# Attention plus soft mixture of experts on one core: the product p v in one PSUM area, the left-over keys in four 64x64 tiles, the keys' factor moved into the maximum's pass, and a plan with every engine strictly in order

## The chip, the core and the metric

One core of one Trainium2 chip runs the whole program. TensorE (PE) multiplies matrices, VectorE (DVE) and ScalarE (ACT) work on tiles, GpSimd (POOL) takes small helpers, and SyncE (SP) issues the DMAs. Results of TensorE land in PSUM, everything else lies in SBUF. The metric is the device time of one execution in microseconds; the median of three runs counts.

## The reference

The inputs are q, k and v of shape (8, 8, 576, 64): 8 batches of 8 heads. Attention keeps only the scores near each row's maximum, and its output, laid out as 4608 rows of 512, goes through a soft mixture of 8 experts with 4 slots each.

```python
scores = scale * q @ k.T                       # scale = 1/8
thresh = max(scores) - tau
scores = where(scores >= thresh, scores, -1e9)
attn = exp(scores - max(scores)); attn /= sum(attn) + 1e-9
x = attn @ v                                   # (4608, 512)
logits = x @ phi                               # 32 slots
d = softmax of logits over the rows;  slot_input = d.T @ x
slot_out[e] = relu(slot_input[e] @ w1[e]) @ w2[e]
out = (softmax of logits over the slots) @ slot_out
```

## The kernel before

**Pairs.** Two heads make a pair: 32 pairs, four to a batch. The head dimension is 64, so the two contraction halves of TensorE's array hold 64 rows each. A pair has nine score blocks (i = 0 to 8): eight of 128 queries of one head against its 576 keys, and a ninth with the last 64 queries of both heads. Line 552 issues a score block as two matmuls side by side, keys 0 to 287 in the upper and 288 to 575 in the lower half of the array (plan mode HALVES); line 557 issues the ninth as four matmuls of 64x64 tiles (mode QUADS).

**A block's way.** The keys have been multiplied by 1/8 (and by 0, if tau is negative) in SBUF by POOL (line 532; for the first pair by DVE in two halves). DVE's pass over the scores in PSUM (line 564) writes the negated scores to SBUF (ss) and accumulates the row's minimum of them (nmx, minus the maximum). ACT takes the exponential (574), POOL the threshold (577), and DVE's second pass (580) zeroes what lies under the threshold, and sums the row. TensorE transposes the result p in 64-row pieces (478, from the helper `ptr`), and ACT copies the transposed pieces to SBUF (483, from `act_copy`): pTa for queries 0 to 255, pTb for 256 to 575, pTl for the 64 left-over keys (512 to 575) of both heads.

**The product p v.** Line 670 makes it in two visits, one for pTa (256 columns) and one for pTb (320 columns). A visit has five steps for each head, the two heads side by side in column halves of the array (mode COLS): four of 128 keys, and a fifth, from pTl, in which 64 rows of vv are zeros, since pTl holds both heads' left-over keys in its 128 partitions. Each visit writes a PSUM area of its own; ACT copies it to xT, TensorE transposes that to x (`ptr`), POOL divides by the row sums (689), and TensorE transposes it back (694). After four pairs `dispatch` makes logits (752) and slot inputs (800, 805) for the batch.

**Areas.** PSUM is cut into four areas ps0 to ps3 of two banks; a score block, a block of transposes and a visit of p v take one each. pTa, pTb, pTl and pL exist once, k, q and vv twice, p2 (two score blocks' p) and ss four times.

**Order.** `Order.add` records every operation with a nominal time (a pair's start plus an entry of OFF or of TABLE), and `plan` turns them into one order per engine by simulating the engines with fixed costs. Before the change, an engine that can't start its first operation by nominal time takes the next one that it can. For TensorE a change of mode costs SWITCH.

**Weights.** 64 units of 512 KB feed the experts. NPRE of them are loaded during the pairs into areas of their own, 20 ("host") into SBUF that the pairs give back at their end, and the rest into areas that the first expert stage has read. SP issues all of them in order.

Of the kernel before, what the change touches and what calls it, by code (L numbers as in the profile page):

```python
# [1174 lines left out]
```

## Time and profile before

| | us |
|---|---|
| median of 3 runs | 548.01 |
| lowest, highest run | 547.24, 548.21 |
| span of the profiled execution, first to last instruction | 546.2 |
| TensorE busy in the span | 527.5 |
| VectorE busy in the span | 471.0 |
| ScalarE busy in the span | 457.4 |
| GpSimd busy in the span | 242.1 |

The profile gives the span of the execution that it took, and no other time of it; the median lies 1.8 us above that span, for what stands before the first and after the last instruction. The granted clock is 1.00 in every stretch until 530 us. From about 20 to 470 us the pairs run, and one batch of four pairs repeats itself every 57.6 us. From 464 to 513 us the weights stream in. A float32 matmul shows as two records, one for each of its two passes, so "x16" in a TensorE row is eight matmuls, that is four of each head.

### The profile page before, as it was taken

What the parts mean: (1) busy time and instruction counts of PE and PEld (TensorE: products, weight loads), DVE (VectorE), ACT (ScalarE), POOL (GpSimd) and SP (SyncE); (2) the same over time, 40 slices, a digit from 0 to 9 for tenths busy, and PEclk for the clock granted to TensorE, in tenths of its full rate; (3) what the DMA queues carried; (4) which work ended last, traced back from release to release, by engine and by line L of the source; (5) the groups of instructions that cost most, each with busy time, mean ns of one, the idle gap of its engine ahead of it and who ended that gap; (6) DMA issues with size and microseconds to landing.
All of it is one profiled execution on the core that took longest, in us unless ns stands there. A gap on an engine that the chain in (4) does not pass through costs nothing.

```text
span 546.2 us, 18324 instructions
## 1 busy us (share of the span) xinstructions
PE 527.5 (97%) x7029; PEld 337.0 (62%) x7029; DVE 471.0 (86%) x1332; ACT 457.4 (84%) x790; POOL 242.1 (44%) x475
## 2 busy tenths in 40 slices
PE   8999999999999999999999999999999999999990
PEld 6666666666666666666666666666666656644470
DVE  5999998999999999999899989999999999523192
ACT  3899998999899989999999989999999888621181
POOL 2554555554545464545355545545454524121030
PEclk9999999999999999999999999999999999999997
DMA  6355555565535543333333333333333322999498
GB/s 176 74 158 178 168 167 169 138 190 161 166 90 167 172 153 122 92 94 86 78 91 92 91 91 92 91 91 91 91 90 91 91 76 69 336 410 408 197 375 316
DMA packets 31990, 83.03 MB, mean 152 GB/s; under 512 B 4640, under 2 KB 12832, under 8 KB 31904
## 3 DMA queue, kind: packets, MB, share of 16 engines
q1 hardware_dynamic: 31904, 81.87, 48.8%
q8 instruction: 55, 0.90, 0.7%
q14 instruction: 31, 0.25, 0.2%
HBM read 72.42 MB, written 9.44 MB: 150 GB/s over the span
## 4 chain that ended last, share of the span: by engine, by line
PE 82%; DVE 5%; DMA 5%; ACT 4%; issue 2%; DVEq 0%; POOL 0%; SPq 0%; POOLq 0%; ACTq 0%
PE ps L670 29%; PE ps L552 24%; PE ps L478 17%; DMA w<-in_w 5%; PE ps L557 3%; PE ps L694 2%; PE ps L752 2%; PE ps L800 1%; DVE p L580 1%; PE up L418 1%; DVE cT L989 1%; DVE host L1086 1%; ACT pTa L483 1%; DVE ss L564 1%; PE ps L470 1%
## 5 line engine op out<-in xcount | busy, mean ns | idle before, releaser
L564 DVE TENSOR_SCALAR_CACHE_REDUCE ss<-ps 128x576 f32<-128x576 f32 x288 | 209.1, 752 | 15.5 <-ACT pTl L483 4.8
L577 POOL TENSOR_SCALAR thr<-nmx,pabs 128x1 f32<-128x1 f32 x288 | 132.2, 461 | 187.0 <-DVE ss L564 167.7
L580 DVE SCALAR_TENSOR_TENSOR p<-ss,thr,p 128x576 f32<-128x576 f32 x256 | 201.8, 823 | 3.4 <-ACT p L574 3.1
L574 ACT ACTIVATE p<-ss,nmx 128x576 f32<-128x576 f32 x256 | 188.2, 781 | 18.3 <-DVE ss L564 18.2
L552 PE MATMUL ps<-k,q 64*128 64x288 f32 x1024 | 167.2, 427 | 1.0 <-ACT pTb L483 0.4
L478 PE MATMUL ps<-ident,p 64*128 64x64 f32 x2304 | 98.2, 223 | 0.9 <-ACT pTa L483 0.3
L478 PEld LDWEIGHTS ps<-ident,p 64*128 64x128 f32 x2304 | 87.8, 138 | 17.8 <-issue 3.3
L552 PEld LDWEIGHTS ps<-k,q 64*128 64x128 f32 x1024 | 83.3, 188 | 21.9 <-ACT pTl L652 5.8
L483 ACT COPY pTb<-ps 128x1024 f32<-128x1024 f32 (+1 forms) x96 | 84.0, 876 | 5.7 <-PE ps L478 3.5
L670 PE MATMUL ps<-pTb,vv 128*64 128x320 f32 x512 | 76.0, 439 | 0.4 <-DVE pTl L652 0.4
L483 ACT COPY pTa<-ps 128x1024 f32<-128x1024 f32 x64 | 64.9, 1018 | 0.4 <-PE ps L478 0.4
L670 PE MATMUL ps<-pTa,vv 128*64 128x256 f32 x512 | 62.3, 385 | 0.0
L670 PEld LDWEIGHTS ps<-pTb,vv 128*64 128x64 f32 x512 | 34.1, 136 | 36.4 <-issue 9.0
L670 PEld LDWEIGHTS ps<-pTa,vv 128*64 128x64 f32 x512 | 33.9, 136 | 26.2 <-DVE ss L564 8.5
L670 PE MATMUL ps<-pTl,vv 128*64 128x256 f32 (+1 forms) x256 | 41.9, 406 | 0.0
L689 POOL TENSOR_TENSOR x<-x,ri 128x512 f32<-128x512 f32 x31 | 32.3, 1043 | 4.8 <-ACT x L483 4.8
L483 ACT COPY xT<-ps 128x256 f32<-128x256 f32 (+1 forms) x62 | 24.6, 398 | 6.2 <-PE ps L670 5.2
L670 PEld LDWEIGHTS ps<-pTl,vv 128*64 128x64 f32 x256 | 18.5, 137 | 12.6
L580 DVE SCALAR_TENSOR_TENSOR pL<-ss,thr,pL 128x576 f32<-128x576 f32 x32 | 26.0, 812 | 0.0
L574 ACT ACTIVATE pL<-ss,nmx 128x576 f32<-128x576 f32 x32 | 24.8, 776 | 0.4 <-DVE ss L564 0.4
L954 POOL TENSOR_TENSOR c<-lall,crow 128x512 f32<-128x512 f32 x9 | 9.3, 1046 | 35.7 <-PE ct L470 21.4
L483 ACT COPY pTl<-ps 128x256 f32<-128x256 f32 x64 | 24.2, 378 | 0.4 <-PE ps L478 0.4
(165 smaller groups left out, 550.3 us busy)
## 6 DMA issues: line engine op xcount, KB each, us to landing
w<-in_w SPq DMA_DIRECT2D x44, 512.0 KB, 7.3
q<-in_qT SPq DMA_DIRECT2D x62, 288.0 KB, 4.5
vv<-in_vt SPq DMA_DIRECT2D x32, 320.0 KB, 4.6
host<-in_w SPq DMA_DIRECT2D x20, 512.0 KB, 7.8
k<-in_kT SPq DMA_DIRECT2D x62, 144.0 KB, 3.0
out<-w SPq DMA_DIRECT2D x8, 512.0 KB, 3.4
out<-host SPq DMA_DIRECT2D x8, 512.0 KB, 5.0
out<-host SPq DMA_DIRECT2D x4, 256.0 KB, 4.6
```

The lines of the kernel that those rows point to most:

```text
L478: nc.tensor.transpose(out=s[:, g, c:c + 64], in_=ins[g], identity=ident[rows[g], rows[g]], tile_position=(64 * g, 0))
L483: G.add("ACT", 51 + 0.833 * n, nom, lambda: nc.scalar.copy(*io()), r, w)
L552: nc.tensor.matmul(s.t[:, g, 0:HS], qt.t[rows[g], h, c * 128:(c + 1) * 128], kt.t[rows[g], h * HS:(h + 1) * HS], start=True, stop=True, ti ...
L557: nc.tensor.matmul(s.t[rows[a], g, 0:HS], qt.t[rows[g], a, SM:S], kt.t[rows[g], a * HS:(a + 1) * HS], start=True, stop=True, tile_position ...
L564: dve(674, t + OFF['mx'], [s], [ss, nmx], lambda s=s, ss=ss, nmx=nmx: nc.vector.tensor_scalar(out=ss.t.rearrange("p (a k) -> p a k", a=2), ...
L574: G.add("ACT", 668, t + OFF['ex'], lambda sv=sv, nmx=nmx, view=view: nc.scalar.activation(view().rearrange("p (a k) -> p a k", a=2), sv(), ...
L577: pool(250, t + OFF['th'], lambda nmx=nmx, thr=thr: nc.gpsimd.tensor_scalar(out=thr.t, in0=nmx.t, scalar1=1.0, scalar2=pabs, op0=ALU.mult, ...
L580: fn=lambda sv=sv, thr=thr, view=view, i=i: nc.vector.scalar_tensor_tensor(out=view().rearrange("p (a k) -> p a k", a=2), in0=sv(), scalar ...
L670: nc.tensor.matmul(lone(w)[h * 64:(h + 1) * 64, 0:n], vv.t[:, v0:v0 + 64], p0, start=(kb == 0), stop=(kb == 4), tile_position=(0, h * 64), ...
L689: G.add("POOL", 1040, u + 6.8, own=f"new{j}", r=[ri[0]], w=[x[j]], fn=lambda: nc.gpsimd.tensor_tensor(out=wide(), in0=wide(), in1=ri.t[:, ...
L694: nc.tensor.transpose(out=w.t[:, g, c * 64:c * 64 + 64], in_=xj()[rows[g], c], identity=ident[rows[g], rows[g]], tile_position=(64 * g, 0))
L752: nc.tensor.matmul(lone(wl)[c * 32:(c + 1) * 32, o], phi_sb[:, k, :], xT[k].t[:, q(c)], start=(k == 0 and not o.start), stop=(k == HP - 1) ...
```

## The change

- **Left-over keys.** The fifth step of p v goes. Instead four matmuls of 64x64 tiles follow the second visit (line 695 of the changed kernel), one for each head and each of two query ranges (256 and 320 columns), in mode QUADS. For that the order of the two heads' left-over keys is swapped for queries from 256 on, keys and p are laid out anew (`kt` is 128 x 2 x 352 now, `at` places a block in p2), and vv's left-over rows are loaded into both halves of the partitions.
- **One area.** Both visits write one PSUM area `o`, one bank each, and it is held from the first visit to the two copies to xT behind the QUADS. pTa and pTb become five slots of pT, one per 128 queries (four used by a pair), and pTL for the last 64 queries: the visits' matmuls have 128 and 64 columns in place of 256 and 320.
- **The factor.** POOL's pass over the keys goes (and DVE's two for the first pair). The maximum's pass multiplies by `nflag8`, a value per partition read from SBUF (minus 1/8, or 0), where it multiplied by the constant -1.0.
- **The plan.** Every engine but SP takes its operations strictly by nominal time. A change of mode costs 92 + 54, and a score behind anything that isn't a score 54 more. The ninth block moves ahead of the last two of the others. All table entries are new.
- **Loads.** A pair's keys come by three DMAs in place of two, its values by three in place of one. NPRE is 25 in place of 26.

```diff
-NPRE = 26
+NPRE = 25
...
-        -279.31, -244.60, -253.66, -174.00, -228.72, -214.94, -219.66, -331.57, -213.22, -305.02, -252.11, -385.08, 317.82, -201.86,
+        -28.68, -46.27, -46.24, -48.35, None, -11.70, -20.09, -3.47, None, 8.91, 2.93, -1.85, 1.91, -4.79, 4.95, 4.82, 4.73,
...
-    k=2, q=2, vv=2, r=3, ri=3, nmx=4, thr=4, p2=4, pL=1, pTa=1, pTb=1, pTl=1, l4=1,
+    k=2, q=2, vv=2, r=3, ri=3, nmx=4, thr=4, p2=4, pL=1, pT=5, pTL=1, pTl=1, l4=1,
...
+                if head[eng] < len(line[eng]):
+                    i = line[eng][head[eng]]
+                    if i in arrived and fits(i, eng):
+                        got = i
+                        head[eng] += 1
...
-                    end += SWITCH * (o[5] != mode) + 50 * (engfree[eng] < t)
+                    end += SWITCH * (o[5] != mode) + LEAD * (o[5] != mode or o[8] and not score) + 50 * (engfree[eng] < t)
...
-            sc = lambda e, kc=kc: lambda: e.tensor_scalar(out=kt.t[:, kc], in0=kt.t[:, kc], scalar1=flag8, **one)
-            if p == 0:
-                G.add("DVE", 370, t0 - 9 + hs[0], sc(nc.vector), [], [kt[h] for h in hs])
-            else:
-                pool(730, t0 - 9, sc(nc.gpsimd), [], [kt[h] for h in hs])
...
             dve(674, t + OFF['mx'], [s], [ss, nmx], lambda s=s, ss=ss, nmx=nmx: nc.vector.tensor_scalar(
-                out=ss.t.rearrange("p (a k) -> p a k", a=2), in0=s.t[:, :, 0:HS], scalar1=-1.0, scalar2=3.4028234663852886e38,
+                out=ss.t.rearrange("p (a k) -> p a k", a=2), in0=s.t[:, :, 0:HS], scalar1=nflag8, scalar2=3.4028234663852886e38,
                 op0=ALU.mult, op1=ALU.min, accum_out=nmx.t))
...
-                for kb in range(5):
-                    for h in range(2):
-                        v0, p0 = ((h * 4 + kb) * 64, pT.t[:, h, kb, :]) if kb < 4 else (SM + h * 64, pTl.t[:, q])
-                        nc.tensor.matmul(
-                            lone(w)[h * 64:(h + 1) * 64, 0:n], vv.t[:, v0:v0 + 64], p0,
-                            start=(kb == 0), stop=(kb == 4), tile_position=(0, h * 64), skip_group_check=True)
+        o = Buf("s")
+        for cs in ((0, 1), (2, 3, 4)):
+            part = [(pT[c], c, 128, c % 2 * 128) if c < 4 else (pTL, c, SL, 256) for c in cs]
+
+            def mm(part=part, k=cs[0] // 2):
+                for z, c, n, m in part:
+                    for kb in range(4):
+                        for h in range(2):
+                            nc.tensor.matmul(
+                                o.t[rows[h], k, m:m + n], vv.t[:, (h * 4 + kb) * 64:][:, 0:64], z.t[:, h, kb, :],
+                                start=(kb == 0 and not m), stop=False, tile_position=(0, h * 64), skip_group_check=True)
...
+        def mm():
+            for k in range(2):
+                for h in range(2):
+                    q = slice(0, QA) if k == 0 else slice(QA, S)
+                    g = h ^ k
+                    nc.tensor.matmul(
+                        o.t[rows[h], k, 0:q.stop - q.start], vv.t[rows[g], SM + h * 64:][:, 0:64], pTl.t[rows[g], q],
+                        start=False, stop=True, tile_position=(64 * g, 64 * h), skip_group_check=True)
```

TensorE's order at the second visit of p v in a pair in the middle of the run, from the first visit on, before. L670 is p v, L552 a score block, L478 transposes, L694 the transposes of x back, and ps0 to ps3 are the PSUM areas:

```order
L670 MATMUL ps2_337<-pTa0_244,vv1_200 64x256 x8
L670 MATMUL ps2_337<-pTl0_208,vv1_200 64x256 x2
L552 MATMUL ps0_335<-k0_312,q0_316 128x288 x2
L478 MATMUL ps1_336<-ident_61,xT0_180 128x64 x8
L552 MATMUL ps2_337<-k0_312,q0_316 128x288 x2
L552 MATMUL ps3_338<-k0_312,q0_316 128x288 x2
L478 MATMUL ps1_336<-ident_61,p22_284 128x64 x16
L552 MATMUL ps0_335<-k0_312,q0_316 128x288 x2
L670 MATMUL ps2_337<-pTb0_204,vv1_200 64x320 x8
L670 MATMUL ps2_337<-pTl0_208,vv1_200 64x320 x2
L694 MATMUL ps0_335<-ident_61,x0_152 128x64 x8
L478 MATMUL ps1_336<-ident_61,p22_284 128x64 x2
```

The same place now, from the second half of the first visit to the transposes of xT. L684 is p v, L695 the four left-over matmuls, L569 a score block, L481 transposes:

```order
L684 MATMUL ps2_352<-pT1_295,vv1_199 64x128 x8
L569 MATMUL ps0_350<-k0_331,q0_335 128x288 x2
L569 MATMUL ps1_351<-k0_331,q0_335 128x288 x2
L481 MATMUL ps3_353<-ident_61,p22_255 128x64 x16
L684 MATMUL ps2_352<-pT0_207,vv1_199 64x128 x8
L684 MATMUL ps2_352<-pT4_223,vv1_199 64x128 x8
L684 MATMUL ps2_352<-pTL0_215,vv1_199 64x64 x8
L695 MATMUL ps2_352<-pTl0_203,vv1_199 64x256 x2
L695 MATMUL ps2_352<-pTl0_203,vv1_199 64x320 x2
L481 MATMUL ps0_350<-ident_61,p21_231 128x64 x16
L569 MATMUL ps1_351<-k1_311,q1_315 128x288 x2
L481 MATMUL ps2_352<-ident_61,xT1_183 128x64 x8
```

The area ps2 now holds the product through both visits and is taken again by the transposes of xT a block of transposes and a score block later; before, it was free between the visits and took a score block there.

VectorE's order where a pair begins, before. L564 is the maximum's pass, L580 the second pass, L618 the reciprocals of the row sums:

```order
L564 TENSOR_SCALAR ss3_196,nmx2_264<-ps2_337 128x576
L618 RECIPROCAL ri2_304<-ri2_304 128x8
L564 TENSOR_SCALAR ss0_216,nmx0_268<-ps1_336 128x576
L564 TENSOR_SCALAR ss2_252,nmx3_300<-ps3_338 128x576
L564 TENSOR_SCALAR ss1_240,nmx1_256<-ps2_337 128x576
L580 SCALAR_TENSOR_TENSOR p22_284,r0_308<-ss3_196,thr2_248,p22_284 128x576
```

And now (L581 is the maximum's pass, L597 the second pass):

```order
L581 TENSOR_SCALAR ss1_275,nmx3_287<-ps2_352,nflag8_78 128x576
L581 TENSOR_SCALAR ss2_243,nmx0_307<-ps0_350,nflag8_78 128x576
L581 TENSOR_SCALAR ss0_267,nmx2_303<-ps2_352,nflag8_78 128x576
L597 SCALAR_TENSOR_TENSOR p22_255,r0_319<-ss1_275,thr3_291,p22_255 128x576
L581 TENSOR_SCALAR ss3_195,nmx1_299<-ps0_350,nflag8_78 128x576
L581 TENSOR_SCALAR ss1_275,nmx3_287<-ps2_352,nflag8_78 128x576
```

The maximum's pass has a second input, nflag8, and a pair's first scores take turns on two areas, ps2 and ps0, where they took three.

## Rows read from the trace of the kernel before

**Rows 1.** The page's span and busy times: time, share of the span, instructions.
```profile
span 546.2 us, 18324 instructions
PE 527.5 (97%) x7029; PEld 337.0 (62%) x7029; DVE 471.0 (86%) x1332; ACT 457.4 (84%) x790; POOL 242.1 (44%) x475
```

**Rows 2.** Busy time by stretch, one batch of pairs and two stretches of the end: stretch, its length, busy time (instructions) of TensorE, its weight loads, VectorE, ScalarE and GpSimd, then granted clock, DMA share and GB/s.
```profile
297.20:354.80 57.60, 57.57 (x820) 37.45 (x818) 54.91 (x158) 54.57 (x95) 28.95 (x56) 1.00 0.34 86
470.00:490.00 20.00, 19.23 (x265) 10.82 (x263) 6.33 (x26) 5.75 (x15) 3.63 (x19) 1.00 1.02 404
490.00:510.00 20.00, 20.00 (x208) 7.83 (x204) 4.29 (x12) 3.37 (x8) 2.05 (x2) 1.00 1.03 410
```

**Rows 3.** The page's chain of work that ended last, as shares of the span: by engine, then by engine, tile and line.
```profile
PE 82%; DVE 5%; DMA 5%; ACT 4%; issue 2%; DVEq 0%; POOL 0%; SPq 0%; POOLq 0%; ACTq 0%
PE ps L670 29%; PE ps L552 24%; PE ps L478 17%; DMA w<-in_w 5%; PE ps L557 3%; PE ps L694 2%; PE ps L752 2%; PE ps L800 1%; DVE p L580 1%; PE up L418 1%; DVE cT L989 1%; DVE host L1086 1%; ACT pTa L483 1%; DVE ss L564 1%; PE ps L470 1%
```

**Rows 4.** TensorE in order of time, a pair and a half in the middle of the run, then two later rows of the same kind: start, duration, line, operation, tiles, array tile and shape, records. A group's own length is best read as the step from its start to the next group's start, since the duration includes the way of the last columns through the array.
```profile
242.84 2.37 PE L670 MATMUL ps<-pTb,vv 128*64 128x320 f32 x16
245.04 0.71 PE L670 MATMUL ps<-pTl,vv 128*64 128x320 f32 x4
245.68 0.46 PE L694 MATMUL ps<-ident,x 64*128 64x64 f32 x8
...
246.60 0.70 PE L552 MATMUL ps<-k,q 64*128 64x288 f32 x4
247.14 0.65 PE L478 MATMUL ps<-ident,p 64*128 64x64 f32 x16
247.63 1.68 PE L552 MATMUL ps<-k,q 64*128 64x288 f32 x12
249.14 0.47 PE L478 MATMUL ps<-ident,pL 64*128 64x64 f32 x10
...
249.58 0.70 PE L552 MATMUL ps<-k,q 64*128 64x288 f32 x4
250.21 1.95 PE L670 MATMUL ps<-pTa,vv 128*64 128x256 f32 x16
251.99 0.60 PE L670 MATMUL ps<-pTl,vv 128*64 128x256 f32 x4
252.52 0.71 PE L478 MATMUL ps<-ident,p 64*128 64x64 f32 x16
...
253.95 0.72 PE L557 MATMUL ps<-k,q 64*64 64x288 f32 x8
254.60 1.24 PE L552 MATMUL ps<-k,q 64*128 64x288 f32 x8
...
289.11 0.71 PE L670 MATMUL ps<-pTl,vv 128*64 128x320 f32 x4
...
302.66 0.71 PE L670 MATMUL ps<-pTl,vv 128*64 128x320 f32 x4
```

**Rows 5.** VectorE in order of time where it doesn't wait: the maximum's pass and the second pass, start and duration.
```profile
279.40 0.75 DVE L564 TENSOR_SCALAR_CACHE_REDUCE ss<-ps 128x576 f32<-128x576 f32 x1
...
280.08 0.75 DVE L564 TENSOR_SCALAR_CACHE_REDUCE ss<-ps 128x576 f32<-128x576 f32 x1
...
280.76 0.81 DVE L580 SCALAR_TENSOR_TENSOR p<-ss,thr,p 128x576 f32<-128x576 f32 x1
...
281.50 0.81 DVE L580 SCALAR_TENSOR_TENSOR p<-ss,thr,p 128x576 f32<-128x576 f32 x1
```

**Rows 6.** Three VectorE instructions of one element per partition at the program's start, each by its line: duration in ns (smallest, median, largest). Lines 392 and 409 have constants alone; line 407 (`scalar2=tau_sb`) reads a value per partition.
```profile
L392 DVE TENSOR_SCALAR flag<-tau_sb x1: 153/153/153, 3.3 to 3.3; 128x1 f32<-128x1 f32 x1
L407 DVE TENSOR_SCALAR nabs<-tau_sb x1: 203/203/203, 3.4 to 3.4; 128x1 f32<-128x1 f32 x1
L409 DVE TENSOR_SCALAR pabs<-nabs x1: 153/153/153, 3.6 to 3.6; 128x1 f32<-128x1 f32 x1
```

**Rows 7.** Groups of instructions by line and shape: out and in (partitions x elements), count, then busy us, mean ns of one, and the engine's idle time before them. Lines 1058 and 1063 both take two tensors of 256 columns; 1063 (`scalar=neg`) also reads a value per partition.
```profile
L564 DVE TENSOR_SCALAR_CACHE_REDUCE ss<-ps 128x576 f32<-128x576 f32 x288 | 209.1, 752 | 15.5 <-ACT pTl L483 4.8 <-PE ps L552 4.2 <-ACT pTa L483 1.9
...
L532 POOL TENSOR_SCALAR k<-k,flag 128x576 f32<-128x576 f32 x31 | 24.2, 780 | 0.7 <-DMA k<-in_kT 0.3
...
L1063 DVE SCALAR_TENSOR_TENSOR sh<-sh,neg,sr 128x256 fp32r<-128x256 f32 x2 | 1.0, 481 | 0.7 <-ACT sh L1062 0.6
...
L532 DVE TENSOR_SCALAR k<-k,flag 128x288 f32<-128x288 f32 x2 | 0.7, 370 | 2.7 <-DMA k<-in_kT 2.7
...
L1058 DVE TENSOR_TENSOR so_sb<-h00e,so_sb 128x256 f32<-128x256 f32 x1 | 0.4, 425 | 9.4 <-issue 9.4
```

**Rows 8.** SP's issues of weight loads at the end of the run: start, time from first to last of the group, line, number.
```profile
453.82 18.90 SPq L460 DMA_DIRECT2D host<-in_w  x12
475.39 5.39 SPq L458 DMA_DIRECT2D host<-in_w  x6
485.40 18.39 SPq L460 DMA_DIRECT2D w<-in_w  x18
```

**Rows 9.** Four pieces of the chain that ended last, in order of time: start, length, what.
```profile
39.28 0.74 DVE p L580 x2
...
439.49 0.82 DVE p L580 x3
...
503.45 10.09 DMA w<-in_w
...
513.58 0.83 PE h00e L1032 x9
```

More of the change, by code (lines that the diff above doesn't have):

```diff
@@ L28 @@
 HALVES, COLS, COLS4, QUADS, WHOLE = range(5)
-SWITCH = 145
+SWITCH = 92
+LEAD = 54
 REGIONS = 4
-NPRE = 26
+NPRE = 25
 UP = 22
@@ L166, in skip, with add @@
         self.where[2] += n
-    def add(self, eng, dur, nom, fn, r=(), w=(), after=(), mode=HALVES, more=0, port=False, own=None):
+    def add(self, eng, dur, nom, fn, r=(), w=(), after=(), mode=HALVES, more=0, port=False, own=None, score=False):
         i = len(self.ops)
@@ L192, in add @@
                 self.newest[x.kind] = i
-        self.ops.append((eng, dur, fn, sorted(deps), list(bufs), mode, more, port))
+        self.ops.append((eng, dur, fn, sorted(deps), list(bufs), mode, more, port, score))
     def plan(self, table):
@@ L249, in plan, with loose, fits @@
         pend = {e: [] for e in engs}
-        mode = None
+        mode, score = None, False
         held = 0.0
+        arrived = set()
+        def loose(i):
+            return ops[i][0] == "SP" or ops[i][0] == "PE" and self.noms[i][0] == "load"
+        line = {e: sorted((i for i in range(n) if ops[i][0] == e and not loose(i)), key=lambda i: (nom[i], i)) for e in engs}
+        head = dict.fromkeys(engs, 0)
+        def fits(x, eng):
+            need = [b.kind for b in ops[x][4] if b.kind is not None and b not in slot]
+            if any(room(k) < need.count(k) for k in need):
+                return False
+            late = [clear(slot[b][0], eng) for b in ops[x][4] if b.kind == "w" and b in slot]
+            if "w" in need and half(t) is None:
+                late.append(min(clear(g, "PE") for g, u in enumerate(region) if 2 not in u and len(u) < 2))
+            if max(late, default=0.0) > t:
+                heapq.heappush(ev, (max(late), 2, -1))
+                return False
+            return True
         ev = [(0.0, 1, i) for i in range(n) if left[i] == 0]
@@ L521, in pair @@
         for hs in parts:
-            kc, n = slice(hs[0] * HS, (hs[-1] + 1) * HS), len(hs)
             def keys(a=hs[0], z=hs[-1] + 1):
-                for g in range(2):
-                    nc.sync.dma_start(
-                        kt.t[rows[g]].rearrange("p (h k) -> p h k", h=2)[:, a:z],
-                        kT[b, j, :, 0:2 * S].rearrange("d (h g k) -> d g h k", h=2, g=2)[:, g, a:z])
-            G.add("SP", 1340 if p else 700, t0 - 18 + hs[0], keys, w=[kt[h] for h in hs])
+                for g, at, n, c, step in ((0, SL, HS, 0, S + SL), (1, 0, KW, HS - SL, S + SL), (0, 0, SL, SM, SL)):
+                    if z - a > 1:
+                        x = kT[b, j, :, c:c + n]
+                        x = bass.AP(x.tensor, x.offset, [x.ap[0], [step, 2], x.ap[-1]])
+                    elif at == 0 and g == 0:
+                        continue
+                    else:
+                        if a and not g:
+                            at, n, c = 0, KW, -SL
+                        c += a * (S + SL)
+                        x = kT[b, j, :, c:c + n].unsqueeze(1)
+                    nc.sync.dma_start(kt.t[rows[g], a:z, at:at + n], x)
+            if hs == (0,):
+                G.add("ACT", 600, t0 - 18, lambda: nc.scalar.dma_start(
+                    kt.t[rows[0], 0:1, 0:SL], kT[b, j, :, SM:S].unsqueeze(1)), w=[kt["l"]])
+            G.add("SP", 1900 if p else 1220, t0 - 18 + hs[0], keys, w=[kt[h] for h in hs])
             for g in range(2):
@@ new lines, in pair @@
+        for cs in ((0, 1), (2, 3, 4)):
[7 more added lines that the diff above has]
+                                start=(kb == 0 and not m), stop=False, tile_position=(0, h * 64), skip_group_check=True)
+            G.add("PE", sum(8 * (4 + 0.834 * x[2]) for x in part), u + OFF['pv'][cs[0] // 2], mm, [x[0] for x in part] + [vv],
+                  [o[cs[0] // 2], xT["t"]], mode=COLS)
@@ new lines, in mm @@
+        def mm():
+            for k in range(2):
+                for h in range(2):
+                    q = slice(0, QA) if k == 0 else slice(QA, S)
[3 more added lines that the diff above has]
+                        start=False, stop=True, tile_position=(64 * g, 64 * h), skip_group_check=True)
+        G.add("PE", 540, u + OFF['pv'][1] + .08, mm, [pTl[0], pTl[2], pTl["L", 0], pTl["L", 1], vv], [o[0], o[1]], mode=QUADS)
@@ L692, in pair @@
             w = Buf("s")
-            G.add("PE", 248, u + 7, own=f"new{j}", r=[x[j]], w=[w], fn=lambda w=w: [
+            G.add("PE", 248, u + 8.6, own=f"new{j}", r=[x[j]], w=[w], fn=lambda w=w: [
                 nc.tensor.transpose(out=w.t[:, g, c * 64:c * 64 + 64], in_=xj()[rows[g], c],
@@ L696, in pair @@
                 for c in range(4) for g in range(2)])
-            G.add("ACT", 477, u + 7.3, own=f"new{j}", r=[w], w=[xT[0], xT[1]], fn=lambda w=w: nc.scalar.copy(
+            G.add("ACT", 477, u + 8.9, own=f"new{j}", r=[w], w=[xT[0], xT[1]], fn=lambda w=w: nc.scalar.copy(
                 xT.t[:, 0:SM].rearrange("p (c g q) -> p g c q", c=4, g=2),
```

178 lines of the change are left out of this document (83 added, 95 removed), and 78 rows, old and new, of the table TABLE.

## The prediction

> **What bounds the kernel now.** I read the chain of waits first: 82% of the span runs over TensorE, and the product p v alone (line 670) is 29% of it, more than the scores (24%) and the transposes of p (17%) [rows 3]. Then the busy times by stretch: in a batch of four pairs TensorE is busy 57.57 of 57.60 us, at the full clock, so nothing that another engine does costs time there. But VectorE is busy 54.91 us and ScalarE 54.57 us of the same stretch [rows 2]: whoever takes more than some 2.7 us of a batch from TensorE alone, or adds as much to VectorE alone, gets another bound. At the end of the run the picture changes: from 470 to 510 us the DMA share is 1.02 to 1.03 at 404 to 410 GB/s [rows 2], the last weight load is issued at 503.45 us, and the chain waits 10.09 us for it [rows 8, 9]. There the bytes still to come set the end. The span is 546.2 us [rows 1] and the median of the runs 548.01; I work out a difference and put it on the median, since what lies outside the span (1.8 us) isn't touched.
>
> **Left-over keys: what TensorE saves.** A visit of p v is 2.20 us for 320 columns (242.84 to 245.04) and 1.78 us for 256 (250.21 to 251.99) [rows 4], eight passes each. The 64 columns between them cost 0.42 / 8 = 0.053 us a pass, so a pass of 320 columns is 0.267 us, one of 256 is 0.213, and some 0.07 us a visit are left for starting it. The fifth step, which goes, is 0.64 us behind the wide visit and 0.53 behind the narrow one; two passes of it are 0.53 and 0.43, so 0.10 us is the price of leaving the mode. Together a pair spends 2.20 + 0.64 + 1.78 + 0.53 = 5.15 us on p v.
>
> Afterwards the first visit has 16 passes of 128 columns (0.107 us each), the second 16 of 128 and 8 of 64 (0.053): 1.71 and 2.14 us, with 0.07 for starting, about 0.05 for the many more passes and 0.10 for leaving each: 1.93 and 2.35. The four left-over matmuls run as two passes of 320 columns, 0.53 us, if all four go side by side as the four of the ninth score block do: that takes 0.65 us for 288 columns (253.95 to 254.60 [rows 4]), 0.48 of passes and 0.17 for the mode. So 0.70 us here. The sum is 4.98 us, 0.17 us less a pair, 0.7 us a batch. The short passes of 64 columns may not hide their weight loads; the eight passes of the nearest rows are transposes, 16 records in 0.49 us (247.14 to 247.63 [rows 4]), 0.061 a side-by-side pair, which would add 0.06 us a pair. That is the lower end of the saving.
>
> **The new order.** By the two orders a batch has 32 changes of mode in place of 27, four of them the step from p v to the left-over matmuls, already counted; the fifth costs 0.15. In return 15 scores in place of 20 follow a transpose. Such a score takes 0.54 us (246.60 to 247.14) where three in a row take 1.51 (247.63 to 249.14), 0.54 + 2 x 0.485 [rows 4]: 0.055 us saved five times, 0.27. TensorE's own work falls by 0.7 + 0.27 - 0.15, about 0.8 us a batch, from 57.62 (245.04 to 302.66 [rows 4]) to 56.8, and a pair without a dispatch from 13.55 (289.11 to 302.66) to 13.3.
>
> **The keys' factor: what VectorE pays.** POOL's pass over the keys (31 of 780 ns [rows 7]) goes. POOL is busy half of a batch [rows 2] and holds nobody up, so that gains nothing in the pairs; the first pair's two passes on VectorE (370 ns each [rows 7]) go too, of which I take 0.2 us. But the maximum's pass now reads a value per partition. The trace has that price twice: of three instructions of one element, the two with constants take 153 ns and the one that reads tau takes 203 [rows 6]; of two that take two tensors of 256 columns, the one with a scalar read per partition takes 481 ns and the other 425 [rows 7]. So 50 to 56 ns more each. It is not hidden behind the instruction before: in a row without waits the maximum's pass starts every 0.68 us (279.40 to 280.08) and the second pass, which has such a scalar, every 0.74 us (280.76 to 281.50), for the same 576 columns [rows 5]. I take 0.06 us, nine times a pair: 0.54 us a pair and 288 times, 17 us, in the whole run. Its lower bound is 0, if a source in PSUM hides the read; its upper bound the 0.06.
>
> The Trainium skill (VectorE: DVE Perf Modes, The TRN2 errata) prices an instruction by its source and its columns, with no term for a scalar read per partition. By it the pass would stay as it is and the time would be that of the first rival; rows 6 speak against it.
>
> **The two together.** VectorE's nine and nine passes took 9 x 0.68 + 9 x 0.74 = 12.8 us a pair beside TensorE's 13.55; now they take 13.3, with two reciprocals 13.4 to 13.5, beside TensorE's 13.3. So in a pair without dispatch VectorE becomes the later one by 0.1 to 0.2 us. In the batch as a whole it has 54.91 + 36 x 0.06 = 57.1 us of busy time (an upper value: before each wait it counts 0.07 us that a following instruction would overlap) against TensorE's 56.8. Its lag can be made up only during the dispatch, 3.4 us of TensorE's (57.62 - 4 x 13.55) with little for VectorE. How a lag reaches TensorE is in the order: a pair's first and third scores both take ps2, so the third waits for the maximum's pass of the first, and behind it on TensorE stand all later scores and transposes. ScalarE has the same copies and exponentials as before. I take it that two or three pairs of a batch run at VectorE's 13.5 and the others at TensorE's pace with 0.1 us of waits: of the 0.8 us a batch 0.4 to 0.6 are given back, 0.2 to 0.4 stay; over some 6.5 undisturbed batches (60 to 440 us) that is 1.3 to 2.6 us, I take 2.0.
>
> **What else.** At both ends of the run the chain already goes over VectorE's passes (39.28 and 439.49 us [rows 9]); there its 0.54 us a pair come on top, two pairs, 1.0 us. One prefetched unit fewer is 0.524 MB more in the stretch that the DMAs set, at some 407 GB/s 1.3 us [rows 2]; but SP's first loads there now wait only for the last pair's keys and queries to be read, not for p, and may start some us earlier: between 0 and 1.3, I take 0.6. The additional small loads of keys and values are issued more than a pair ahead, at a DMA share of 0.34 [rows 2], and cost nothing as long as they land in time. Sum: -2.0 + 1.0 + 0.6 - 0.2 = -0.6 us, so 547.4, about **547.5 us**.
>
> **Rivals.**
> 1. *VectorE's lag doesn't matter.* Either the scalar is read for nothing, or the dispatch and the four slots of ss take up the lag. Then TensorE's 0.8 us come through in some 7.5 batches, 6.0 us, with 0.6 lost in the tail and 0.2 gained at the start: 542.4. For it: VectorE still waits in a batch today. Against it: rows 5 to 7.
> 2. *VectorE sets every pair.* With the strict order it waits now for TensorE's scores, now for ScalarE's exponentials, and no longer overlaps them with something else. If each pair takes 13.8 us (13.5 and 0.3 us of waits; today it has 15.5 us of idle time ahead of 288 maximum's passes, 0.5 us a pair [rows 7]), 24 pairs lose 0.25 us each, and the ends lose 1: 554. It ends slower, and decides as soon as the waits that stay exceed 0.1 us a pair.
> 3. *The left-over matmuls don't run side by side.* Of the four, the two heads' matmuls for one query range lie in different row halves of the array and write the same bank of `o`; in the ninth score block the two row halves write two banks. If they take turns, a pair pays 0.53 us more, 17 us in all, of which TensorE's saving of 6 pays back part: 559. The Trainium skill (TensorEngine Tiling (Array Packing), Restrictions and Gotchas) says just that different row tiles can't access the same PSUM bank at the same time and that software has to see to it. Here the two write different partitions of the bank, and no row shows that case.
>
> **How the numbers follow.** The likeliest case, 50%: VectorE's price eats most of the saving, 547.5, between 545 and 550.5. Rival 1, 24%: 540 to 544.5. Rival 2, 20%: 551 to 556. Rival 3, 6%: 556 to 562. A measurement of this kernel can tell 0.2% from no change, 1.1 us. Faster by more (under 546.9) are rival 1 and a third of the likeliest, 0.41; the same is somewhat under half of the likeliest, 0.23; slower the rest of it and rivals 2 and 3, 0.36. A range that leaves out rival 3, the lower end of rival 1 and the upper end of rival 2 is 541 to 554.5.
>
> **What would show it.** The row of the maximum's pass at about 810 ns in place of 752, and steps of 0.74 us; at 752, the scalar was free. TensorE's idle time per batch above 0.5 us and ended by VectorE's ss or ScalarE, with VectorE's busy share above TensorE's today; a TensorE still busy throughout would mean rival 1. The two visits at 1.93 and 2.35 us with their leaving, and the left-over matmuls at 0.6 to 0.7 us to the next group; 1.1 or more is rival 3. A batch of 57.2 to 57.4 us. The chain's last wait for weights shifted by no more than 1.3 us against the end of the pairs. I am wrong if TensorE waits for something that I haven't named, above all for the copies to xT, which now stand between the left-over matmuls and the transposes that take the same area 1.0 us later.

## The result, and the profile after

| | before | after |
|---|---|---|
| median, us | 548.21 (5 runs) | 551.11 (5 runs) |
| lowest, highest run, us | 547.24, 548.91 | 550.63, 552.23 |
| span of the profiled execution, us | 546.2 | 549.2 |

The ratio is 1.0056, with an interval of 1.0044 to 1.0069: the changed kernel is slower by 3 us, and the interval lies clear of no change. The forecast was 547.5, in a range of 541 to 554.5.

The page of the changed kernel, against [rows 1]: span, then busy time, share and instructions of each engine.

```profile
span 549.2 us, 21270 instructions
PE 530.6 (97%) x8565; PEld 395.3 (72%) x8565; DVE 480.5 (87%) x1330; ACT 455.2 (83%) x790; POOL 203.6 (37%) x444
```

One batch of four pairs in the middle of the run, by stretch, with the columns of [rows 2]:

```profile
264.52:322.62 58.10, 58.10 (x1014) 45.01 (x1013) 55.97 (x157) 54.21 (x95) 24.17 (x52) 1.00 0.37 92
```

The batch is 0.5 us longer, and TensorE is busy in it from end to end. By this row TensorE never waits, and its own work has grown. The row misleads: the record of a group goes on past the start of the next one (the first below ends at 274.59 us, 0.07 us after the next has begun), so a short wait lies hidden under the records. Such waits show only in the steps from one group's start to the next one's. Here are the second half of a pair and the beginning of the next, TensorE in order of time:

```profile
272.62 1.97 PE L684 MATMUL ps<-pT,vv 128*64 128x128 f32 x32
274.52 1.44 PE L569 MATMUL ps<-k,q 64*128 64x288 f32 x8
275.79 0.66 PE L481 MATMUL ps<-ident,p 64*128 64x64 f32 x16
276.39 1.97 PE L684 MATMUL ps<-pT,vv 128*64 128x128 f32 x32
278.18 0.64 PE L684 MATMUL ps<-pTL,vv 128*64 128x64 f32 x16
278.75 0.77 PE L695 MATMUL ps<-pTl,vv 64*64 64x256 f32 x8
279.45 0.71 PE L481 MATMUL ps<-ident,p 64*128 64x64 f32 x16
279.99 0.70 PE L569 MATMUL ps<-k,q 64*128 64x288 f32 x4
280.53 0.41 PE L481 MATMUL ps<-ident,xT 64*128 64x64 f32 x8
280.78 0.66 PE L481 MATMUL ps<-ident,p 64*128 64x64 f32 x16
281.32 0.76 PE L569 MATMUL ps<-k,q 64*128 64x288 f32 x4
281.91 0.28 PE L481 MATMUL ps<-ident,p 64*128 64x64 f32 x4
282.03 0.71 PE L569 MATMUL ps<-k,q 64*128 64x288 f32 x4
282.73 0.71 PE L481 MATMUL ps<-ident,p 64*128 64x64 f32 x16
283.28 0.70 PE L569 MATMUL ps<-k,q 64*128 64x288 f32 x4
```

The product p v is what was forecast: visits of 1.90 us (272.62 to 274.52) and 1.79 + 0.57 (276.39 to 278.75), the left-over matmuls 0.70 (278.75 to 279.45). But two score blocks behind the first visit take 1.27 us (274.52 to 275.79), where two such blocks can take 1.08 (271.44 to 272.52 in run e1 below), and a single score 0.70 (282.03 to 282.73), where 0.54 is usual (279.99 to 280.53).

**The account of a batch.** I added up all such steps over five batches, and took away what the shortest steps of both kernels show: 62 ns for a side-by-side pair of transposes, 485 for a score block and 553 for the ninth, 93 for leaving to another mode, 50 for the first block behind a change of mode, and 55 for a score that doesn't follow a score. What is left over are waits. In us a batch; "columns" are the scores and transposes without these extras (30.38) and the dispatch (2.75), the same everywhere; "changes" are changes of mode:

| kernel | batch | p v | columns | modes (changes) | first scores | waits |
|---|---|---|---|---|---|---|
| before | 57.73 | 20.61 | 33.13 | 2.23 (27) | 1.27 | 0.49 |
| after | 58.12 | 19.84 | 33.13 | 2.37 (32) | 1.32 | 1.47 |
| with the constant (e1) | 57.68 | 19.84 | 33.13 | 2.37 | 1.32 | 1.02 |
| constant, short x (e5) | 57.23 | 19.84 | 33.13 | 2.37 | 1.32 | 0.57 |
| after, short x (e13) | 58.05 | 19.84 | 33.13 | 2.37 | 1.32 | 1.40 |
| after, two scalars (e14) | 59.50 | 20.16 | 33.13 | 2.37 | 1.32 | 2.53 |
| before, with a scalar (e2) | 58.03 | 20.61 | 33.13 | 2.23 | 1.27 | 0.79 |

(In e14 another 0.32 us of waits lies within p v.) TensorE's own work fell by 0.59 us, its waits rose by 0.98: 0.40 us more a batch, 2.8 us in seven batches, nearly the 3.0 us between the two spans. The row of one batch gave 0.5 us, since two of the five batches before are longer (57.85 and 57.89 us) than the one in [rows 2].

The groups of VectorE's two passes, which answer to [rows 7]: count, busy us, mean ns of one, idle time before.

```profile
L581 DVE TENSOR_SCALAR_CACHE_REDUCE ss<-ps,nflag 128x576 f32<-128x576 f32 x288 | 225.9, 812 | 12.9 <-PE ps L569 8.0 <-issue 4.3
L597 DVE SCALAR_TENSOR_TENSOR p<-ss,thr,p 128x576 f32<-128x576 f32 x256 | 202.4, 817 | 0.2
```

The maximum's pass is 60 ns longer, as forecast. VectorE where the two scores at 274.52 wait for an area, in order of time:

```profile
273.58 0.82 DVE L581 TENSOR_SCALAR_CACHE_REDUCE ss<-ps,nflag 128x576 f32<-128x576 f32 x1
...
274.32 0.82 DVE L581 TENSOR_SCALAR_CACHE_REDUCE ss<-ps,nflag 128x576 f32<-128x576 f32 x1
...
275.06 0.82 DVE L597 SCALAR_TENSOR_TENSOR p<-ss,thr,p 128x576 f32<-128x576 f32 x1
```

Steps of 0.74 us without a gap: VectorE has work queued, and the area that TensorE needs comes free when the pass that began at 274.32 is through.

The end of the run: SP's last issues of weight loads, and the chain's last waits for weights, against [rows 8, 9].

```profile
488.86 18.04 SPq L463 DMA_DIRECT2D w<-in_w  x19
```

```profile
496.15 10.36 DMA w<-in_w
506.57 10.11 DMA w<-in_w
```

The last load is issued 3.1 us later (506.57 against 503.45), and the last pair's left-over matmuls start 2.6 us later (477.20 against 474.58, line 670 there): the end follows the pairs, with 0.5 us on top.

### The profile page after: what moved, and what is told of

The parts are those of the page before. It is cut to its first block, busy times and chain, and to the rows that moved or that the text cites. A ratio compares the mean times of both kernels' runs of the same rounds, so it can differ in the third digit from the quotient of the medians.

```text
span 549.2 us, 21270 instructions
## 1 busy us (share of the span) xinstructions
PE 530.6 (97%) x8565; PEld 395.3 (72%) x8565; DVE 480.5 (87%) x1330; ACT 455.2 (83%) x790; POOL 203.6 (37%) x444
## 4 chain that ended last, share of the span: by engine, by line
PE 84%; DMA 6%; DVE 5%; issue 3%; ACT 1%; POOL 0%; DVEq 0%; SPq 0%; POOLq 0%; ACTq 0%
PE ps L569 26%; PE ps L684 24%; PE ps L481 18%; DMA w<-in_w 5%; PE ps L695 4%; PE ps L574 4%; PE ps L779 2%; DVE p L597 2%; PE ps L827 2%; PE ps L721 1%; DVE ss L581 1%; PE up L421 1%; DVE host L1113 1%; DMA out<-w 1%; PE ps L473 1%
## 5 line engine op out<-in xcount | busy, mean ns | idle before, releaser
L581 DVE TENSOR_SCALAR_CACHE_REDUCE ss<-ps,nflag 128x576 f32<-128x576 f32 x288 | 225.9, 812 | 12.9 <-PE ps L569 8.0
L597 DVE SCALAR_TENSOR_TENSOR p<-ss,thr,p 128x576 f32<-128x576 f32 x256 | 202.4, 817 | 0.2
L594 POOL TENSOR_SCALAR thr<-nmx,pabs 128x1 f32<-128x1 f32 x288 | 115.6, 406 | 210.2 <-DVE ss L581 187.4
L569 PE MATMUL ps<-k,q 64*128 64x288 f32 x1024 | 174.3, 438 | 0.5 <-ACT pT L486 0.2
L486 ACT COPY pT<-ps 128x1024 f32<-128x1024 f32 x128 | 130.4, 1020 | 2.1 <-PE ps L481 2.1
L684 PE MATMUL ps<-pT,vv 128*64 128x128 f32 x2048 | 125.7, 276 | 0.0
L684 PEld LDWEIGHTS ps<-pT,vv 128*64 128x64 f32 x2048 | 110.5, 137 | 7.2 <-ACT xl L486 2.7
L481 PEld LDWEIGHTS ps<-ident,p 64*128 64x128 f32 x2304 | 90.4, 138 | 35.0 <-ACT pT L486 12.7
L481 PE MATMUL ps<-ident,p 64*128 64x64 f32 x2304 | 105.2, 225 | 1.2 <-DVE p L597 0.8
L569 PEld LDWEIGHTS ps<-k,q 64*128 64x128 f32 x1024 | 80.6, 187 | 35.7 <-DVE ss L581 18.7
L628 POOL TENSOR_SCALAR pL<-pL,ri 128x576 f32<-128x576 f32 x31 | 26.8, 864 | 11.7 <-DVE ri L624 11.7
L695 PE MATMUL ps<-pTl,vv 64*64 64x256 f32 (+1 forms) x256 | 25.2, 428 | 0.6 <-issue 0.6
L597 DVE SCALAR_TENSOR_TENSOR pL<-ss,thr,pL 128x576 f32<-128x576 f32 x32 | 25.7, 802 | 0.0
L486 ACT COPY x<-ps 128x512 f32<-128x512 f32 x32 | 18.9, 590 | 6.7 <-PE ps L481 6.7
L581 DVE DVE_READ_ACCUMULATOR ss<-ps,nflag 128x1 f32 x288 | 23.8, 83 | 0.0
L574 PE MATMUL ps<-k,q 64*64 64x288 f32 x256 | 22.9, 428 | 0.0
```

The lines of the kernel that those rows point to most:

```text
L481: nc.tensor.transpose(out=s[:, g, c:c + 64], in_=ins[g], identity=ident[rows[g], rows[g]], tile_position=(64 * g, 0))
L486: G.add("ACT", 51 + 0.833 * n, nom, lambda: nc.scalar.copy(*io()), r, w)
L569: nc.tensor.matmul(s.t[:, g, 0:HS], qt.t[rows[g], h, c * 128:(c + 1) * 128], kt.t[rows[g], h, (h ^ c // 2 ^ 1) * SL:][:, 0:HS], start=True ...
L574: nc.tensor.matmul(s.t[rows[a], g, 0:HS], qt.t[rows[g], a, SM:S], kt.t[rows[g], a, (a ^ 1) * SL:][:, 0:HS], start=True, stop=True, tile_po ...
L581: dve(674, t + OFF['mx'], [s], [ss, nmx], lambda s=s, ss=ss, nmx=nmx: nc.vector.tensor_scalar(out=ss.t.rearrange("p (a k) -> p a k", a=2), ...
L594: pool(250, t + OFF['th'], lambda nmx=nmx, thr=thr: nc.gpsimd.tensor_scalar(out=thr.t, in0=nmx.t, scalar1=1.0, scalar2=pabs, op0=ALU.mult, ...
```

## The experiments

In all runs before stands beside the kernel on the same chip; a ratio is to that. Theory A: the scalar read per partition makes VectorE late. Theory B: the strict order makes the waits. Theory C, added after the first four runs: ScalarE's copies behind the left-over matmuls make them.

**e1: the constant in the maximum's pass.** The case of a negative tau is left out.

```diff
-in0=s.t[:, :, 0:HS], scalar1=nflag8, scalar2=3.4028234663852886e38,
+in0=s.t[:, :, 0:HS], scalar1=-0.125, scalar2=3.4028234663852886e38,
```

> The changed kernel, whose maximum's pass multiplies by the constant -0.125 in place of the value per partition; the case of a negative tau is left out. No order changes. Theory A (the scalar read per partition makes VectorE late, and TensorE pays for it in short waits that lie under its records, 1.48 us of a batch where the kernel before has 0.45): the pass goes back from 812 to about 752 ns, the batch from 58.13 to 57.1 to 57.3 us, the time to 543 to 546. Theory B (the waits come from the strict order and from the area that p v now holds through both visits): the pass is at 752 ns all the same, but the batch stays at 57.9 to 58.2 us and the time at 549.5 to 551.

Measured: 547.02, ratio 0.9982 (0.9969 to 0.9995); the batch at 57.68, the pass at 751 ns:

```profile
L581 DVE TENSOR_SCALAR_CACHE_REDUCE ss<-ps 128x576 f32<-128x576 f32 x288 | 208.3, 751 | 20.9 <-ACT x L486 11.0 <-PE ps L569 8.7 <-issue 0.2
```

The changed kernel stands at 1.0056, so the scalar costs 0.74% or 4.1 us, by the two intervals give or take 1 us. In the two traces, whose spans differ by 4.2 us, 1.7 of it lie ahead of the first dispatch (80.21 us against 78.53), 2.7 between the first and the seventh (six batches of 0.45), and -0.2 behind that. But A alone had 543 to 546: 1.02 us of waits stay. The same score blocks behind the first visit as shown above, in this run:

```profile
269.55 1.97 PE L684 MATMUL ps<-pT,vv 128*64 128x128 f32 x32
271.44 1.24 PE L569 MATMUL ps<-k,q 64*128 64x288 f32 x8
272.52 0.66 PE L481 MATMUL ps<-ident,p 64*128 64x64 f32 x16
...
278.04 0.76 PE L569 MATMUL ps<-k,q 64*128 64x288 f32 x4
278.63 0.28 PE L481 MATMUL ps<-ident,p 64*128 64x64 f32 x4
278.75 0.70 PE L569 MATMUL ps<-k,q 64*128 64x288 f32 x4
279.45 0.71 PE L481 MATMUL ps<-ident,p 64*128 64x64 f32 x16
```

1.08 us (271.44 to 272.52) in place of 1.27: that wait was VectorE's, since only its pass is shorter. The score at 278.75 still takes 0.70: that one isn't.

**e2: the kernel before, with a scalar.** A value per partition of -1.0 in place of the constant.

```diff
-in0=s.t[:, :, 0:HS], scalar1=-1.0, scalar2=3.4028234663852886e38,
+in0=s.t[:, :, 0:HS], scalar1=mone, scalar2=3.4028234663852886e38,
```

> The kernel before, whose maximum's pass reads its factor (-1.0) from a value per partition; nothing else changes. Theory A: the pass goes to 812 ns here too, 36 times 0.06 us are 2.1 us of a batch, and VectorE has 2.7 us of room in a batch by its busy time; it gets late in places, so the batch grows by 0.3 to 1.5 us and the time to 550 to 558. Theory B: the loose plan and the free areas take it up, and the time stays within 1.1 us of 548.2.

Measured: 551.62, ratio 1.0060 (1.0043 to 1.0077); the pass 808 ns, the batch 58.03, waits 0.79. So A holds in the old order too: of 2.1 us more for VectorE, 0.3 a batch reach TensorE.

```profile
L566 DVE TENSOR_SCALAR_CACHE_REDUCE ss<-ps,mone 128x576 f32<-128x576 f32 x288 | 223.6, 808 | 8.4 <-PE ps L554 2.8 <-ACT pTa L485 1.7 <-issue 1.3
```

**e3, e7, e10: the factor back on GpSimd.** The constant -1.0 in the maximum's pass, and the keys multiplied ahead, in one pass of 704 columns (e3), in two of 352 (e7), or in one at a place where GpSimd had a hole (e10).

```diff
+            kc = slice(hs[0], hs[-1] + 1)
+            sc = lambda e, kc=kc: lambda: e.tensor_scalar(out=kt.t[:, kc], in0=kt.t[:, kc], scalar1=nflag8, **one)
...
+                pool(900, t0 - 4, sc(nc.gpsimd), [], [kt[h] for h in hs])
```

In e10 that line has `t0 + (-3.0, -2.705, 1.4, -1.45)[j]`; in e7 it is two passes, at t0 - 4 and t0 - 2.5.

> The changed kernel with the keys' factor alone undone: GpSimd multiplies the keys again (704 columns with the new layout, about 0.95 us a pair; for the first pair VectorE does it in two halves), and the maximum's pass multiplies by -1.0. Theory A: 543.5 to 546.5, the time of the run with the constant and 0.3 to 0.6 us for the first pair's passes. Theory B: 550 to 552. If GpSimd's passes hold up its thresholds in the strict order, some 0.3 us a pair come on top under both, 8 to 10 us in all.

> The run with GpSimd's pass over the keys, cut into two passes of 352 columns 1.5 block times apart. If the long pass (1.05 us) held up the thresholds that GpSimd makes for VectorE: two of about 0.55 us fit between them, the batch falls from 58.53 towards the 57.68 of the run with the constant, 57.7 to 58.0, and the time from 554.0 to 547.5 to 549.5. If the price is GpSimd's work as such, beside VectorE's passes: the batch stays above 58.3 us, and the time at 552 to 554.

> The run with GpSimd's pass over the keys, placed in each kind of pair where GpSimd had a hole of over 2 us in the trace of the run with the constant, and not ahead of the pass over pL. If the price of the pass (58.53 against 57.68 us a batch) is what it holds up on GpSimd: 57.7 to 57.9 us a batch and 548 to 549.5. If it is the slowing of VectorE's passes beside a busy GpSimd: 58.2 us or more, 551 to 554.

Measured: 553.99 (1.0100), 554.86 (1.0129) and 553.77 (1.0102), all slower than the changed kernel. In e3 the transposes of pL waited for GpSimd's pass over pL, behind the new pass. In e7 half the columns aren't half the price:

```profile
L547 POOL TENSOR_SCALAR k<-k,nflag 128x352 f32<-128x352 f32 x62 | 46.6, 752 | 0.3 <-PE ps L576 0.2
```

Two of 752 ns in place of one of 1052, by the means. These mix two cases: the shortest passes take 547 ns for 352 columns and 843 for 704, and those that meet a second pass of VectorE's up to 1137 and 1431. In e10 the pass has a hole on GpSimd, and the price shows on VectorE. GpSimd and VectorE at the same time in e10:

```profile
272.95 0.84 POOL L547 TENSOR_SCALAR k<-k,nflag 128x704 f32<-128x704 f32 x1
```

```profile
271.06 0.81 DVE L602 SCALAR_TENSOR_TENSOR p<-ss,thr,p 128x576 f32<-128x576 f32 x1
...
273.15 1.25 DVE L602 SCALAR_TENSOR_TENSOR p<-ss,thr,p 128x576 f32<-128x576 f32 x1
274.33 0.81 DVE L602 SCALAR_TENSOR_TENSOR p<-ss,thr,p 128x576 f32<-128x576 f32 x1
```

The second pass beside GpSimd's takes 1.25 us in place of 0.81; over the run its mean is 873 ns (816 in e1). GpSimd takes from VectorE nearly what the scalar did (8 times 0.057 against 9 times 0.06 us a pair). The slowed passes end 0.60 us after GpSimd's pass, whether they began 0.04 us before it (1.49 us), 0.20 (1.25) or 0.30 us (1.16) behind: VectorE's pass waits for GpSimd's. That this is the whole price in e10 (a batch of 58.48 us against 57.68 in e1) is argued and not shown. So GpSimd's pass isn't free here, though GpSimd is idle most of the time.

**e4: the sign in the exponential,** with the constant -0.125 in the maximum's pass.

```diff
-AF.Exp, bias=nmx.t, scale=-1.0),
+AF.Exp, bias=nmx.t, scale=nflag8),
```

> The changed kernel with the constant -0.125 in the maximum's pass, and the sign of tau in the exponential on ScalarE instead, whose scale is read per partition (minus 1, or 0 for a negative tau, for which the threshold is put out of reach). Theory A, and a scale that ScalarE reads for nothing (782 ns stay): 543 to 546 like the run with the constant. If the scale costs ScalarE what the scalar cost VectorE, 36 times 0.055 are 2.0 us of a batch, ScalarE is busy 56.2 of 57.2 us, and 546 to 551 come out. Theory B: 549.5 to 551.

Measured: 554.43, ratio 1.0111 (1.0094 to 1.0128). The exponential went from 782 to 876 ns:

```profile
L591 ACT ACTIVATE p<-ss,nmx,nflag 128x576 f32<-128x576 f32 x256 | 215.7, 876 | 8.3 <-DVE ss L581 8.1
```

Here a scale per partition costs ScalarE 94 ns, where a scalar costs VectorE 60. The price was above the one assumed (55), and the time over its upper end.

**e5, e13: a shorter copy of x.** ScalarE copies 128 of 512 columns, beside the constant (e5) and in the changed kernel (e13). The rest of x stays at zero, which GpSimd writes once at the start.

```diff
-            x.t[:, :, j * 128:(j + 1) * 128].rearrange("p c (g d) -> p g c d", g=2),
-            w.t[:, :, 0:256].rearrange("p g (c d) -> p g c d", c=4)))
+            x.t[:, 0:1, j * 128:(j + 1) * 128].rearrange("p c (g d) -> p g c d", g=2),
+            w.t[:, :, 0:64].rearrange("p g (c d) -> p g c d", c=1)))
```

> The run with the constant, in which ScalarE copies only 128 of the 512 columns of x from PSUM (the rest of x is left at zero, and the case of a negative tau is left out); GpSimd clears x once at the start. In the run with the constant 1.02 us of a batch are still short waits of TensorE, 0.3 us in each of three pairs in the 3.5 us behind the left-over matmuls, where ScalarE makes two copies to xT, one of a block of transposes, the copy to x and another block one after the other. Theory C (ScalarE's queue there sets when the areas come free, which the new place of the copies to xT brought): the waits fall to 0.3 to 0.6 us, the batch from 57.68 to 57.1 to 57.3 us, the time from 547.0 to 543 to 545.5. Rival (the waits come from the strict order or VectorE): the batch stays at 57.6 to 57.7 us and the time at 546 to 547.5.

> The changed kernel with its scalar per partition, in which ScalarE copies only 128 of the 512 columns of x (the rest of x stays zero). If VectorE's lag and ScalarE's copies each make their own waits, the 0.45 us a batch that the shorter copy gave beside the constant come here too: 57.6 to 57.8 us a batch, 1.0 to 1.1 us of waits, 548 to 550. If VectorE, late already, sets the same places: 58.0 to 58.15 us, 550.5 to 551.5.

Measured for e5: 545.56, ratio 0.9958 (0.9946 to 0.9971), the batch 57.23. The place shown above, in e5:

```profile
278.04 0.76 PE L569 MATMUL ps<-k,q 64*128 64x288 f32 x4
278.63 0.28 PE L481 MATMUL ps<-ident,p 64*128 64x64 f32 x4
278.75 0.71 PE L569 MATMUL ps<-k,q 64*128 64x288 f32 x4
279.29 0.70 PE L481 MATMUL ps<-ident,p 64*128 64x64 f32 x16
```

and ScalarE's queue there, where the copy of x is now 0.27 us; ahead of it the copy of the same place in the changed kernel:

```profile
281.16 0.59 ACT L486 COPY x<-ps 128x512 f32<-128x512 f32 x1
```

```profile
276.31 0.70 ACT L486 COPY xT<-ps 128x256 f32<-128x256 f32 x2 [0.22 <-PE ps L695]
276.98 1.02 ACT L486 COPY pT<-ps 128x1024 f32<-128x1024 f32 x1
277.89 0.27 ACT L486 COPY x<-ps 128x128 f32<-128x128 f32 x1
278.21 1.01 ACT L486 COPY pT<-ps 128x1024 f32<-128x1024 f32 x1
```

The score at 278.75 takes 0.54 us again: beside the constant that wait is ScalarE's, as C has it. That the new place of the copies to xT brought it isn't shown, as the kernel before wasn't run with the short copy. The time gained less than seven batches of 0.45 us, because clearing x (1.81 us of GpSimd) stands ahead of the making of the identity, and the first score starts at 8.70 us, not 6.91.

Measured for e13: 552.51, ratio 1.0091 (1.0075 to 1.0107), with a first score at 7.83 us, not 6.99; the batch is 58.05, waits 1.40. The place of C lost its wait, and others got it: with the scalar VectorE sets most of the batch's waits, and ScalarE's copies come second.

**e6: the kernel before with NPRE of 25.**

> The kernel before with NPRE of 25: one unit of 512 KB more is loaded in the stretch at the end that the DMAs set, and the pairs' order is the same. If those bytes set the end: 1.3 us more, 549.4 to 549.8. If SP issues them in a hole: within 0.4 us of 548.3.

Measured: 548.25 against 547.86, ratio 1.0005 (0.9996 to 1.0014): at most 0.8 us, nearer to a hole. In its trace the last load is issued 0.9 us later (504.37 against 503.45).

**e8: the old rule of the plan.** The first operation in the list that can start, of the next 40, in place of the first alone.

> The changed kernel with the old rule of the plan: an engine that can't start its first operation by nominal time takes the next one that it can. 88 of 1261 rows of TensorE's order differ, some score blocks moved ahead of a block of transposes. Theory B (the strict order makes the waits): the waits of 1.47 us a batch fall below 1.1, and the time to 547.5 to 549.5. Theories A and C (VectorE's longer pass and ScalarE's copies make them): 1.3 to 1.6 us remain, and 550 to 552.

Measured: 563.52, ratio 1.0285 (1.0271 to 1.0299); waits 2.61 us a batch. The waits grow where theory B had them fall. But the nominal times are those of the strict rule: what the old rule would give with times of its own wasn't tried, and neither was the area that p v holds through both visits by itself.

**e9, e11, e12: the transposes of xT moved.** Beside the constant (e9), with GpSimd's pass in the holes (e11) and in the changed kernel (e12). One of four such lines, one for each kind of pair:

```diff
...
+    ("pair1", 89): 20.95, ("pair2", 37): 12.75, ("new1", 1): 23.00, ("pair1", 90): 21.00, ("new1", 2): 23.90,
...
```

> The run with the constant, with other nominal times at one place of every pair: behind the left-over matmuls the transposes of xT come one block of transposes and one score block later, ScalarE's copy to x one copy later, the two transposes of left-over keys behind the next score block, and the transposes of x back behind the ninth block. No work is left out but the case of a negative tau. Theory C (TensorE waits there because ScalarE's copies follow each other without a score block's time between them): of the 0.31 us a pair 0.2 go, in three or four pairs, the batch falls from 57.68 to 56.9 to 57.2 us, the time from 547.0 to 541.5 to 544.5. If the wait only moves to the next block that needs an area: 57.5 to 57.8 us and 546 to 548.

> Both together, with nothing left out: GpSimd's pass in the holes, and the moved transposes of xT. If theory C holds and the holes hide the pass: 57.0 to 57.4 us a batch, 543 to 546, under both kernels. If one of the two fails: 547 to 549.5; if both: over 551.

> The changed kernel itself, with its scalar per partition, and the moved transposes of xT alone. Theory A with C (VectorE's lag and ScalarE's copies add up): the batch falls from 58.12 by 0.4 to 0.8 us to 57.3 to 57.7, the time from 551.1 to 545.5 to 548.5. If VectorE, now the later engine, takes all of it: 57.9 to 58.1 us, 550 to 551.

Measured: 566.21 (1.0327), 576.21 (1.0518) and 574.50 (1.0480), far outside every expectation. The trace of e9 shows a reason: GpSimd's multiplication of x (L722) had kept its place in GpSimd's strict order.

```profile
257.36 1.04 POOL L722 TENSOR_TENSOR x<-x,ri 128x512 f32<-128x512 f32 x1 [3.89 <-ACT x L492]
258.38 0.50 POOL L600 TENSOR_SCALAR thr<-nmx,pabs 128x1 f32<-128x1 f32 x2
258.86 1.25 POOL L634 TENSOR_SCALAR pL<-pL,ri 128x576 f32<-128x576 f32 x1
```

x came later, GpSimd waited 3.89 us for it with two thresholds and pL queued behind, VectorE waited 0.81 us for a threshold, and TensorE 0.73 us for pL. The runs say nothing on C; they suggest what it costs to move an operation on three queues and not on the fourth. An order that also moves GpSimd's part wasn't tried.

**e14: two scalars in the changed kernel.**

```diff
-scalar1=nflag8, scalar2=3.4028234663852886e38,
+scalar1=nflag8, scalar2=big,
```

> The changed kernel, whose maximum's pass reads its second operand too (the bound of 3.4e38) from a value per partition. Theory A with a price for each scalar read: the pass goes from 812 to 865 to 875 ns, VectorE gets 2.0 us a batch more, and now nearly all of it is TensorE's: the batch grows by 1.3 to 2.1 us to 59.4 to 60.2, the time to 560 to 566. If the price is one for the form of the instruction and not for each scalar: 812 ns, 58.1 us, 551.

Measured: 563.15, ratio 1.0282 (1.0268 to 1.0296); the batch 59.50.

```profile
L583 DVE TENSOR_SCALAR_CACHE_REDUCE ss<-ps,nflag,big 128x576 f32<-128x576 f32 x288 | 243.2, 870 | 8.5 <-PE ps L571 6.2 <-issue 0.3
```

752, 812, 870 ns with no, one and two scalars: the price goes by each. The first costs a batch 0.45 us, the second 1.38.

## Why the prediction was wrong

**The failed step** is "of the 0.8 us a batch 0.4 to 0.6 are given back, 0.2 to 0.4 stay". Both its numbers were off: 0.59 us were saved and 0.98 given back. The time lies within the stated range, but slower than before, where rival 2 begins (551). Rival 2's condition came true, waits above 0.1 us a pair; its price was too high (58.12 / 4 = 14.53 us a pair against 14.43 before, where it had 0.25 more; its own sum, 24 times 0.25 and 1.0 on 548.0, is 555 and not 554). Its cause, VectorE in every pair, is only one part; ScalarE's copies are another.

- *Left-over keys: right.* 19.84 / 4 = 4.96 us a pair, forecast 4.98; visits of 1.90 and 2.36 (1.93 and 2.35), the left-over matmuls 0.70.
- *Rival 3 fell.* The four run side by side in 0.70 us, though two of them write one bank from different row halves. What the Trainium skill (TensorEngine Tiling (Array Packing), Restrictions and Gotchas) says against that isn't seen here, where the two write different partitions of the bank.
- *Changes of mode: right; first scores: wrong.* 32 changes in place of 27 cost 0.14 us, forecast 0.15. But "0.055 us saved five times, 0.27" isn't there: I counted the scores that follow a transpose, and a score behind p v or the ninth block pays its 0.055 as well. There are 24 such scores now, 23 before: 0.05 more. So 0.59 us were saved, not 0.8.
- *The scalar: right in its price.* 60 ns, steps of 0.74 us; e2 and e14 show the same per scalar. The rule of the Trainium skill (VectorE: DVE Perf Modes, The TRN2 errata), which has no term for it, is not borne out.
- *What the scalar does to TensorE: right, 0.45 us a batch by e1.* This is what the sum had for all waits.
- *What was missing.* Without the scalar 1.02 us of waits stay, 0.53 more than before, and e5 puts 0.45 of them on ScalarE's copies behind the left-over matmuls. The sum had nothing for these. The prediction named the place in its last sentence, without a price. Before, the copies to xT came after each visit, half a pair apart; now both follow the left-over matmuls, and three more copies stand behind them. That this made the waits is argued from the orders.
- *The two don't add up.* With the scalar, taking ScalarE's part away gives 0.07 us (e13); with the constant it gives 0.45. VectorE comes first, and when it is relieved ScalarE is next. That is why rival 1 (542.4) didn't come even with the scalar free: e1 is at 547.02.
- *The ends: the tail right, the rest not.* Start -0.2, both ends +1.0 and the tail +0.6 were forecast, together +1.4; the spans leave 0.2 for them beside the batches' 2.8. To the last pair's left-over matmuls the kernels differ by 2.6 us, no more than the batches, so the two ends cost nothing on balance; e1's trace puts the scalar's price outside the batches at the start alone. The tail costs 0.5 us (3.1 - 2.6), near the 0.6. One prefetched unit fewer is 0.4 us in e6, by its medians, within its interval of none.

The version with the constant beats both kernels, but isn't the whole computation. Of the whole ones among the runs, with the factor on GpSimd (e3, e7, e10) or its sign on ScalarE (e4), none came under the changed kernel.

## What to carry to other kernels

An engine that is busy from end to end in the profile may still wait: add up the steps between the starts of its groups, take away the shortest ones, and the rest are waits with a place and a releaser. A saving on the bounding engine was worth no more here than the room that the others had, each at its own place, and the second in line showed only when the first was relieved; so price every one of them before the change. When an operation is moved in a strict order, look at every queue that it passes: in e9 what stood behind it on the one that kept its place had to wait.
